# Later eviction of the sum banks that share a tile, stores on GpSimd's queue, and V's bound in two steps, in a fused attention and expert-layer kernel

## The chip, the cores and the metric

The kernel runs on one core of a Trainium2 chip. The metric is the device time of one execution in microseconds (us). TensorE (PE) does the matrix products, VectorE (DVE) and ScalarE (ACT) everything elementwise, SyncE (SP) and GpSimd (POOL) issue transfers. Each engine works through its own list of instructions in order, and waits on semaphores for the others.

## The reference

```python
def _attn_ref(q, k, v, proj):                      # 4 batches, 8 heads, 768 rows, 64 columns
    q_bits = (np.einsum('bhsd,dk->bhsk', q, proj) > 0)
    k_bits = (np.einsum('bhsd,dk->bhsk', k, proj) > 0)
    mask = q_bucket[:, :, :, None] == k_bucket[:, :, None, :]
    scores = np.where(mask, scale * np.matmul(q, k.transpose(0, 1, 3, 2)), -1000000000.0)
    attn = np.exp(scores - np.max(scores, axis=-1, keepdims=True))
    attn = attn / (np.sum(attn, axis=-1, keepdims=True) + 1e-09)
    return np.matmul(attn, v)

def _moe_ref(x, w_in, w_out):                      # 3072 x 512, 512 x 2048, 2048 x 512
    h = x @ w_in
    g = np.where(h > 0.0, h, np.exp(np.minimum(h, 0.0)) - 1.0)
    return g @ w_out
```

The attention's output, heads side by side, is the input of the two products. The weights are 64-bit floats in memory and are decoded by the kernel.

## The kernel before

**Tiling.** The rows of a batch make two chunks of 384 rows (three blocks of 128), eight chunks in all. Heads go in four pairs. A slot of the main loop is one query tile: 128 rows of one head, so a pair has six slots in a chunk, a chunk 24, a batch 48. Every number that enters a product is split into a high and a low half in float16, and three products replace one.

**One slot.** PE makes the scores of a query tile (`s`, L507, four matmuls). DVE copies them out with their row maximum (`pt`, L519); only then is the one score tile `s` free again. For each two query tiles ACT makes the exponentials (L535) and the high half of the normalised rows (`hl`, L143), DVE the low half (L152), and SP issues transfers that transpose them into `PT` (L550). Some slots later PE multiplies them with V (`av`, L558). In the steps of the loop that are due then, ACT, DVE and SP also prepare Q, K and V for later pairs; the bits of the buckets come from small products (`z`, L286).

**The two weight products run one chunk behind, between the scores.** `moe_stream` yields one matmul at a time. `first` makes `h` for 128 of the 2048 inner columns (f = 0 to 15; 12 matmuls, L584); ACT and DVE make `U`, the activated halves (L595, L598, L599, L143, L152). `second` adds one f to the sums of the chunk's three row blocks (L620, three matmuls for each block). The sums are in three PSUM banks for the whole chunk: `o[0]` and `o[1]` are the two halves of one tile named `o`, `o[2]` is a tile of its own, `o2`. After the last f, each block's sum is scaled into an SBUF tile `ot`, a slice of `W` (`W<-o` in the profile; the first and third block on ACT at L143, the second on DVE at L145), and stored to `out_dram` (L632). There are two `ot` slices for the three blocks, so the third block's copy waits until the first block's store has landed.

**What orders the work.** PE's list is the order in which the code is written. ACT's, DVE's and SP's lists are set by a scheduler that places each instruction by priority; the copies of the sums have high priority. Instructions that touch one tile in conflict are ordered by the tile, not by the half of it.

**V's bound.** For each batch after the first, V is loaded, its four parts are squared and summed on ACT (L207), and one step `scale` takes the largest sum (L411, DVE), multiplies it with ones on PE to spread it over partitions (`sum<-vx`, L184), and makes a scale from it in five small DVE instructions (L186 to L199). Four steps `split` then write V's halves (`vhl`, two instructions on ACT, two on DVE each). The steps are due at slots counted from the batch's first slot.

Of the kernel before, what the change touches and what calls it, by code (L numbers as in the profile page):

```python
# [19 lines left out]
V_TOP = 13  # L20
# [46 lines left out]
def lsh_attention_moe(  # L67
# [55 lines left out]
    def part(name):  # L123

        n = taken.get(name, 0)
        taken[name] = n + 1
        return area[name][n % len(area[name])]
# [43 lines left out]
    def behind_max():  # L171
        return tc.issue_after(latest[-1].ins) if latest else nullcontext()

    def powers(mx, n, floor, top, tag, pool=None, rows=False, squares=False, ex=None):

        pool = pool or small  # L180
        mall = pool.tile([P, n], F32, tag=tag + "m", name=tag + "m")
        if not rows:
            t = ps_a.tile([P, 512], F32, tag="av", name="sum")[:, :n]
            nc.tensor.matmul(t, ones, mx.bitcast(BF16).rearrange("p (n t) -> p n t", t=2)[:, :, 1], start=True, stop=True)  # L184
            mx = t
        nc.vector.tensor_scalar(mall, mx, floor, None, ALU.max)  # L186
        if ex is None:
            ex = pool.tile([P, n], F32, tag=tag + "e", name=tag + "e")
        if squares:

            nc.vector.tensor_scalar(
                ex.bitcast(I32), mall.bitcast(I32), 1, 0x7F800000, ALU.logical_shift_right, ALU.bitwise_and
            )
            nc.vector.tensor_scalar(ex, ex, 2.0**64, None, ALU.mult)
        else:
            nc.vector.tensor_scalar(ex.bitcast(I32), mall.bitcast(I32), 0x7F800000, None, ALU.bitwise_and)
        sc = pool.tile([P, n], F32, tag=tag + "s", name=tag + "s")
        nc.vector.reciprocal(sc, ex)
        nc.vector.tensor_scalar(sc, sc, 2.0**top, None, ALU.mult)  # L199
        return ex, sc  # L200
# [182 lines left out]
    def prep_v(b):  # L383
        st = {"f": [], "v": [None] * NP}

        def load():
            mx = small.tile([P, NP], F32, tag="vx", name="vx")
            for p in range(NP):
                f = vpool.tile([P, 2, NC, D], F32, tag="v", name="vf")
                with tc.issue_after(ks[b, V_AFTER]["done"].ins) if b == 0 else nullcontext():  # L390
                    nc.sync.dma_start(
                        f.rearrange("p h c d -> p h (c d)"),
                        v[b, 2 * p : 2 * p + 2].rearrange("h (p c) d -> p h (c d)", c=NC),
                    )
                st["f"].append(f)
            st["mx"] = mx
            if b == 0:
                for p in range(NP):
                    sums(p)

        def sums(p):
            f = st["f"][p]
            squares(st["mx"][:, p : p + 1], f.rearrange("p h c d -> p (h c d)"), steady.k1 if b else junk0)

        def scale():
            with behind_max():
                bound()

        def bound():
            m1 = small.tile([P, 1], F32, tag="vx1", name="vx1")  # L410
            nc.vector.tensor_reduce(m1, st["mx"], axis=AX.X, op=ALU.max)  # L411
            st["ex"], st["sc"] = powers(m1, 1, 2.0**-34, V_TOP, "v", squares=True)

        def split(p):
            f = st["f"][p]
            t = vpool.tile([P, 2, NC, 2, D], F16, tag="v", name="vhl")
            st["v"][p] = t
            for j in range(2):
                scaled("v_hi", t[:, j, :, 0, :], f[:, j], st["sc"])
                rest("v_lo", t[:, j, :, 1, :], f[:, j], st["sc"], t[:, j, :, 0, :])  # L420

        parts = [lambda p=p: sums(p) for p in range(NP)] if b else []
        return st, [load] + parts + [scale] + [lambda p=p: split(p) for p in range(NP)]


    wst = {}
# [145 lines left out]
    def moe_stream(chunks):  # L572
# [33 lines left out]
        def second(c, f, g16):  # L606
            n = c["nc"]
            if f == 0:
                if not banks:
                    two = ps_o.tile([P, 2, 512], F32, tag="o", name="o")  # L610
                    banks.extend([two[:, 0], two[:, 1], ps_o.tile([P, 512], F32, tag="o2", name="o2")])
                c["o"] = banks[:n]
                c["os"] = small.tile([P, 1], F32, tag="os", name="os", bufs=2)
                nc.vector.scalar_tensor_tensor(
                    c["os"], vs[c["b"]][0]["ex"], 2.0 ** (G_DOWN - V_TOP - 2 * W_TOP), wst["e2"], ALU.mult, ALU.mult
                )
            o = c["o"]
            for t in range(n):
                for i, (gx, wx) in enumerate(((0, 0), (0, 1), (1, 0))):
                    nc.tensor.matmul(  # L620
                        o[t][:, :DO],
                        g16[:, gx, t * P : (t + 1) * P],
                        WH[:, NSI + 1 + f, wx, :],
                        start=f == 0 and i == 0,
                        stop=f == NF - 1 and i == 2,
                    )
                    if f == NF - 1 and i == 2:
                        rows = out[c["b"] * S : (c["b"] + 1) * S, :].rearrange("(p c) o -> p c o", c=NC)
                        ot = part("ot")
                        with tc.high_priority():  # L630
                            scaled("out", ot, o[t][:, :DO], c["os"])
                        nc.sync.dma_start(rows[:, c["c0"] + t, :], ot)  # L632
                    yield DO

        for c in chunks:
# [140 lines left out]
        vs[b] = prep_v(b)  # L776
    for b in range(1, B):
        s0 = [c for c in chunks if c["b"] < b][-1]["end"]
        vdue += [(s0 + x, s) for x, s in zip((-16, -14, -13, -12, -11, -9, -8, -2, 4, 10), vs[b][1])]


    wq = list(wsplits)
# [50 lines left out]
    def weights(n):  # L833
        nonlocal w_credit, w_at
        w_credit += n
        while w_credit >= 1:

            at = (w_at + (2 if w_at >= NSI else 1)) * SL
            users = {x[1] for x in due} | ({"v"} if len(vdue) == NP + 2 + (B - 1) * (2 * NP + 2) else set())
            if any(a < at + SL and at < z and users & u for a, z, u in guards):  # L840
                break
            if w_at not in w64 and w_at < NSI + NSO:
                break
            w_credit -= 1
            if w_at >= W_SPLIT and NSI not in split_done and len(split_done) < KT:
                split_w()
            elif w_at < NSI + NSO:
                wdecode(w_at)
                w_at += 1
                load_w()  # L850
                if w_at in (NSI, NSI + NSO):
                    wscale(w_at // (NSI + NSO))
            elif wq:
                split_w()
# [97 lines left out]
```

## Time and profile before

| | |
|---|---|
| median of 3 runs | 966.19 us (963.73 to 966.58) |
| the profiled execution | 964.54 us |
| its span, first to last instruction | 962.7 us |
| PE, ACT, DVE busy | 825.0, 742.0, 705.7 us |
| mean granted clock of PE | 0.95 |

The profile is of one execution, and its span is 1.84 us shorter than its own time. A group of instructions is named by its line, its engine and its tiles, out<-in. "Idle before" is the time in which the engine had nothing to do ahead of the instruction, with the instruction whose end released it. "PEclk" is the share of full speed that PE's clock was granted.

### The profile page before, as it was taken

The page shows a single profiled execution, that of the slowest core. Times are in us where ns is not written, and L with a number is a line of the kernel's source. Part 1 is how long each engine was busy: PE and PEld are TensorE (multiplying, and loading weights), DVE is VectorE, ACT ScalarE, POOL GpSimd, SP SyncE. Part 2 cuts the span into 40 slices and gives each one's busy share as a digit, 9 for nine tenths or more (in the row PEclk, how much of TensorE's full clock was granted, in tenths as well). Part 3 has the DMA queues.
Part 4 walks back from the last instruction along what each step waited for, and adds up shares of the span by engine and source line. Part 5 has one row for each costly group of instructions (what it writes and reads, how often), then busy time and mean ns, then how long its engine had stood idle before and what let it go on. Part 6 is the DMA issues. An engine that isn't in the chain of part 4 may idle for free.

```text
span 962.7 us, 14525 instructions
## 1 busy us (share of the span) xinstructions
PE 825.0 (86%) x4975; PEld 422.4 (44%) x4975; DVE 705.7 (73%) x1528; ACT 742.0 (77%) x1469; POOL 2.6 (0%) x25
## 2 busy tenths in 40 slices
PE   2536555879989999889989998989989999999997
PEld 0113222434445555444545554544545454555453
DVE  6789899898877777678767686687877687665232
ACT  5667777999879787789779797698878788786443
POOL 1000000000000000000000000000000000000000
PEclk9998665999999999899999999999999999999999
DMA  9999988676886759486887666785786767656000
GB/s 284 264 201 215 223 213 179 131 151 139 158 177 151 151 107 144 97 186 120 166 188 135 127 130 122 136 165 102 143 168 126 125 116 149 100 99 99 33 1 33
DMA packets 406121, 138.46 MB, mean 144 GB/s; under 512 B 380960, under 2 KB 398880, under 8 KB 406048
## 3 DMA queue, kind: packets, MB, share of 16 engines
q1 hardware_dynamic: 405888, 137.54, 69.4%
q8 instruction: 39, 0.64, 0.3%
q14 instruction: 34, 0.28, 0.1%
q10 hardware_dynamic: 160, 0.00, 0.0%
HBM read 35.65 MB, written 6.29 MB: 44 GB/s over the span
## 4 chain that ended last, share of the span: by engine, by line
PE 55%; DVE 16%; DMA 15%; ACT 8%; issue 4%; SPq 1%; ACTq 0%; DVEq 0%
PE o L620 18%; PE h L584 18%; PE av L558 9%; PE s L507 7%; DVE pt L519 4%; DMA O<-nat1q 3%; DVE hl L152 3%; DMA K<-natk 3%; DMA PT<-hl 3%; ACT pt L535 3%; PE z L286 2%; ACT W L143 1%; DMA W<-in_moe_w_in_dram 1%; DVE U L152 1%; DVE natk L152 1%
## 5 line engine op out<-in xcount | busy, mean ns | idle before, releaser
L620 PE MATMUL o<-W,U 128*128 128x512 f16 x1152 | 283.8, 384 | 20.0 <-ACT W L143 20.0
L584 PE MATMUL h<-x,W 128*128 128x384 f16 x1536 | 284.1, 329 | 0.0
L584 PEld LDWEIGHTS <-W 128*128 128x128 f16 x1536 | 148.2, 98 | 123.8 <-issue 24.0
L519 DVE TENSOR_SCALAR_CACHE_REDUCE pt<-s 128x768 f32<-128x768 f32 x177 | 168.2, 950 | 42.8 <-PE s L507 41.6
L535 ACT ACTIVATE pt<-pt,nb,sg 128x768 f32<-128x768 f32 x192 | 195.3, 1019 | 1.8
L152 DVE SCALAR_TENSOR_TENSOR hl<-pt,r,hl 128x768 f16<-128x768 f32 x192 | 189.9, 1011 | 9.2 <-ACT hl L143 8.9
L143 ACT ACTIVATE hl<-pt,r 128x768 f16<-128x768 f32 x192 | 168.6, 926 | 32.7 <-DVE r L545 32.1
L620 PEld LDWEIGHTS <-U 128*128 128x128 f16 x1152 | 111.8, 98 | 141.6 <-issue 28.4
L507 PE MATMUL s<-K,O 128*128 128x384 f16 x708 | 152.7, 339 | 19.0 <-DVE pt L519 15.1
L558 PE MATMUL av<-PT,vhl 128*64 128x384 f16 x1152 | 114.9, 353 | 26.4 <-DMA PT<-hl 13.7
L599 DVE SCALAR_TENSOR_TENSOR U<-U 128x384 f32<-128x384 f32 x128 | 70.8, 553 | 79.5 <-ACT U L598 79.2
L507 PEld LDWEIGHTS <-O 76*128 76x128 f16 (+1 forms) x768 | 74.8, 102 | 120.5 <-issue 42.1
L595 ACT ACTIVATE U<-h,ch 128x384 f32<-128x384 f32 x128 | 73.1, 571 | 66.8 <-PE h L584 66.3
L152 DVE SCALAR_TENSOR_TENSOR U<-U,sgg 128x384 f16<-128x384 f32 x128 | 78.4, 613 | 53.8 <-ACT U L143 53.8
L558 PEld LDWEIGHTS <-vhl 128*64 128x64 f16 x1152 | 73.2, 118 | 80.4 <-issue 16.3
L143 ACT ACTIVATE U<-U,sgg 128x384 f16<-128x384 f32 x128 | 77.8, 608 | 25.5 <-DVE U L599 25.4
L598 ACT ACTIVATE U<-h,ch 128x384 f32<-128x384 f32 x128 | 72.9, 570 | 0.0
L471 PE MATMUL acc<-W,ones 128*128 128x512 bf16 x32 | 17.0, 547 | 34.8 <-DVE W L468 33.9
L535 ACT ACTIVATION_READ_ACCUMULATOR pt<-pt,nb,sg 128x1 f32 x192 | 36.3, 189 | 0.0
L291 DVE TENSOR_SCALAR zb<-z,pjt 64x384 f16<-64x384 f32 (+1 forms) x48 | 29.1, 606 | 6.9 <-PE z L286 6.9
L532 ACT ACTIVATE nb<-m,sg 128x2 f32<-128x2 f32 x96 | 27.7, 288 | 5.4 <-DVE pt L519 4.9
L286 PE MATMUL z<-O,pjz 64*32 64x384 f16 (+1 forms) x192 | 27.5, 363 | 2.4 <-DVE w0m L186 1.7
(102 smaller groups left out, 502.7 us busy)
## 6 DMA issues: line engine op xcount, KB each, us to landing
U<-in_moe_w_in_dram SPq DMA_DIRECT2D x12, 512.0 KB
vf<-in_v_dram SPq DMA_DIRECT2D x16, 384.0 KB
U<-in_moe_w_out_dram SPq DMA_DIRECT2D x12, 512.0 KB
out_dram<-W SPq DMA_DIRECT2D x24, 256.0 KB
qst<-in_q_dram SPq DMA_DIRECT2D x30, 192.0 KB
kst<-in_k_dram SPq DMA_DIRECT2D x14, 384.0 KB
PT<-hl SPq DMA_TRANSPOSE x192
W<-in_moe_w_in_dram SPq DMA_DIRECT2D x4, 512.0 KB
```

The lines of the kernel that those rows point to most:

```text
L143: nc.scalar.activation(o, x, AF.Copy, scale=s)
L152: nc.vector.scalar_tensor_tensor(o, x, s, hi, ALU.mult, ALU.subtract)
L286: nc.tensor.matmul(t[u * QD : (u + 1) * QD], pj["z"][:rows, x, :], mv, start=n == 0, stop=n == len(ways) - 1)
L507: nc.tensor.matmul(s_tile[:, n, :HALF], st[o][:rows, at, :], kst[kk][:rows, j * NC + n * HC : j * NC + (n + 1) * HC, :].rearrange("p a b - ...
L519: top = nc.vector.tensor_scalar(pt.rearrange("p (n e) -> p n e", n=2), s_tile[:, :, :HALF], CLAMP, None, ALU.max, ALU.max, accum_out=duo[0 ...
L535: nc.scalar.activation(pt, pt, AF.Exp, bias=nb[:, n : n + 1], scale=st["sg"][:, 0:1], accum_out=sm[:, n : n + 1])
L558: nc.tensor.matmul(av[j * D : (j + 1) * D], vt[:, j, c, vx, :], PTs[j][:, :, px, c, :], start=n == 0, stop=n == last,)
L584: nc.tensor.matmul(h, WH[:, g * KT + t, wx, fc * P : (fc + 1) * P], c["xs"][t][:, xx, :], start=n == 0, stop=n == 3 * KT - 1,)
L595: nc.scalar.activation(e, h, AF.Exp, scale=c["ch"])
L598: nc.scalar.activation(hp, h, AF.Relu, scale=c["ch"])
L599: nc.vector.scalar_tensor_tensor(e, e, -1.0, hp, ALU.add, ALU.min)
L620: nc.tensor.matmul(o[t][:, :DO], g16[:, gx, t * P : (t + 1) * P], WH[:, NSI + 1 + f, wx, :], start=f == 0 and i == 0, stop=f == NF - 1 and ...
```

## The change

```diff
         def scale():
             with behind_max():
-                bound()
-
-        def bound():
-            m1 = small.tile([P, 1], F32, tag="vx1", name="vx1")
-            nc.vector.tensor_reduce(m1, st["mx"], axis=AX.X, op=ALU.max)
-            st["ex"], st["sc"] = powers(m1, 1, 2.0**-34, V_TOP, "v", squares=True)
+                st["ex"], st["sc"] = powers(st["m1"], 1, 2.0**-34, V_TOP, "v", squares=True)
...
+        def top():
+            m1 = small.tile([P, 1], F32, tag="vx1", name="vx1")
+            with behind_max():
+                nc.vector.tensor_reduce(m1, st["mx"], axis=AX.X, op=ALU.max)
+            st["m1"] = m1
...
-        return st, [load] + parts + [scale] + [lambda p=p: split(p) for p in range(NP)]
+        return st, [load] + parts + ([top, scale] if b else [lambda: (top(), scale())]) + [lambda p=p: split(p) for p in range(NP)]
...
-                    if f == NF - 1 and i == 2:
-                        rows = out[c["b"] * S : (c["b"] + 1) * S, :].rearrange("(p c) o -> p c o", c=NC)
-                        ot = part("ot")
-                        with tc.high_priority():
-                            scaled("out", ot, o[t][:, :DO], c["os"])
-                        nc.sync.dma_start(rows[:, c["c0"] + t, :], ot)
+                    if f == NF - 1 and i == 2 and (t > 0 or n == 1):
+                        for u in range(t + 1) if t < 2 else (2,):
+                            rows = out[c["b"] * S : (c["b"] + 1) * S, :].rearrange("(p c) o -> p c o", c=NC)
+                            ot = part("ot")
+                            with tc.high_priority():
+                                scaled("out", ot, o[u][:, :DO], c["os"])
+                            nc.gpsimd.dma_start(rows[:, c["c0"] + u, :], ot)
...
-        vdue += [(s0 + x, s) for x, s in zip((-16, -14, -13, -12, -11, -9, -8, -2, 4, 10), vs[b][1])]
+        vdue += [(s0 + x, s) for x, s in zip((-16, -14, -13, -12, -11, -9, -7, -5, 1, 6, 11), vs[b][1])]
...
-            users = {x[1] for x in due} | ({"v"} if len(vdue) == NP + 2 + (B - 1) * (2 * NP + 2) else set())
+            users = {x[1] for x in due} | ({"v"} if len(vdue) == NP + 2 + (B - 1) * (2 * NP + 3) else set())
```

The first block's sum is no longer copied out between the last matmuls of the first block and those of the second: both are copied after the second block's last matmul, the third after its own. All 24 stores are issued by POOL instead of SP. The step that takes V's largest sum stays nine slots ahead of the batch; the product with ones and the scale follow two slots later, and the four splits are due at slots -5, 1, 6 and 11 instead of -8, -2, 4 and 10.

At the end of the fourth chunk, ACT's list around the copies of the sums (`W<-o`: the copy from tile `o`; `W<-o_1559`: from tile `o2`; `U`: the activated halves; `hl`, `r`, `nb`, `pt`: the query tiles) was:

```order
L207 ACTIVATE nat1q,qx<-qst 128x384
L143 ACTIVATE hl<-pt,r 128x768 x2
L143 ACTIVATE W<-o,os 128x512
L143 ACTIVATE U<-U,sgg 128x384
L532 ACTIVATE nb<-m,sg 128x2
L535 ACTIVATE pt,sm<-pt,nb,sg 128x768 x2
L544 ACTIVATE r<-sm 128x2
L143 ACTIVATE hl<-pt,r 128x768 x2
L595 ACTIVATE U<-h,ch 128x384
L598 ACTIVATE U<-h,ch 128x384
L143 ACTIVATE W<-o_1559,os 128x512
```

and is now, from the same `nat1q` on:

```order
L207 ACTIVATE nat1q,qx<-qst 128x384
L143 ACTIVATE hl<-pt,r 128x768 x2
L143 ACTIVATE U<-U,sgg 128x384
L143 ACTIVATE W<-o,os 128x512
L533 ACTIVATE nb<-m,sg 128x2
L536 ACTIVATE pt,sm<-pt,nb,sg 128x768 x2
L596 ACTIVATE U<-h,ch 128x384
L599 ACTIVATE U<-h,ch 128x384
L545 ACTIVATE r<-sm 128x2
L143 ACTIVATE W<-o_1559,os 128x512
L596 ACTIVATE U<-h,ch 128x384
L599 ACTIVATE U<-h,ch 128x384
```

The copy of the first sum stays where it was, but for one instruction; a pair of `U` instructions now stands ahead of the second `hl` pair, and so does the copy from `o2`. On DVE at the same place (`W<-o`: the copy of the second block's sum; `zb`: bits of the buckets) before:

```order
L519 TENSOR_SCALAR pt,m<-s 128x768
L152 SCALAR_TENSOR_TENSOR hl<-pt,r,hl 128x768 x2
L152 SCALAR_TENSOR_TENSOR U<-U,sgg 128x384
L145 TENSOR_SCALAR W<-o,os 128x512
L291 TENSOR_SCALAR zb<-z,pjt 64x384
L545 RECIPROCAL r<-r 128x2
L519 TENSOR_SCALAR pt,m<-s 128x768
```

and now:

```order
L520 TENSOR_SCALAR pt,m<-s 128x768
L152 SCALAR_TENSOR_TENSOR hl<-pt,r,hl 128x768
L291 TENSOR_SCALAR zb<-z,pjt 64x384
L152 SCALAR_TENSOR_TENSOR hl<-pt,r,hl 128x768
L152 SCALAR_TENSOR_TENSOR U<-U,sgg 128x384
L145 TENSOR_SCALAR W<-o,os 128x512
L520 TENSOR_SCALAR pt,m<-s 128x768
```

`zb` moved ahead of the copy, and the next score tile is taken right behind it, ahead of a reciprocal. PE's list is the same in both kernels, except for the product of V's largest sum with ones. For the third batch it stood inside the twelve matmuls of one `h`:

```order
L584 MATMUL h<-x_3447,W 128x384
L184 LDWEIGHTS ones
L184 MATMUL sum<-vx_4260,ones 128x1
L584 LDWEIGHTS W
L584 MATMUL h<-x_3447,W 128x384
```

and stands now 72 matmuls later, after the next `av`, two score tiles and an `h`:

```order
L621 MATMUL o<-W,U 128x512
L184 LDWEIGHTS ones
L184 MATMUL sum<-vx_4260,ones 128x1
L621 LDWEIGHTS U
L621 MATMUL o<-W,U 128x512
```

On DVE the maximum itself keeps its place, behind the same score tile; only what follows the product moved back by some ten instructions.

## Prediction

> **What bounds the kernel now.** The page comes first, for the span and the engines' shares:
>
> ```profile
> span 962.7 us, 14525 instructions
> ...
> PE 825.0 (86%) x4975; PEld 422.4 (44%) x4975; DVE 705.7 (73%) x1528; ACT 742.0 (77%) x1469; POOL 2.6 (0%) x25
> ...
> PEclk9998665999999999899999999999999999999999
> ```
>
> No engine is full over the whole span, so the share alone decides nothing. The view of stretches, asked for the time between two chunk ends, does:
>
> ```profile
> 302.00:384.00 82.00, 82.00 (x525) 44.33 (x520) 61.35 (x131) 67.54 (x136) 0.00 (x0) 1.00 0.75 132
> ```
>
> The columns are the stretch, its length, then PE, weight loads, DVE, ACT and POOL busy, PE's clock, the DMA share and GB/s. PE is busy in all 82.00 us at full clock; ACT lacks 14.5 us and DVE 20.7. There PE is the bound, and what it loses elsewhere it can't win back here. So the waits of PE after the start-up, 200 us to the end, are what a change can gain:
>
> ```profile
> PE o L620 <- ACT W L143: 20.0, 8, 5.2
> PE s L507 <- DVE pt L519: 9.9, 15, 1.2
> PE sum L184 <- DVE vx L411: 9.2, 3, 3.9
> PE av L558 <- DMA PT<-hl: 3.6, 2, 2.1
> PE av L558 <- DMA O<-zb: 2.0, 1, 2.0
> ```
>
> These are total, times and longest. The first is the second block's matmuls held by the copy of the first block's sum, once in each chunk; the third is the product with V's largest sum, once for each batch after the first. Together they are 29.2 of 44.7 us, and the change aims at both. They cost more than their idle time. Of the half-clock stretches after 200 us, every one begins during such a wait or just behind it:
>
> ```profile
> 213.66:220.49 6.83, 5.87 (x28) 2.67 (x29) 5.55 (x15) 6.36 (x13) 0.00 (x0) 0.50 0.94 249
> ...
> 387.75:394.57 6.82, 5.00 (x16) 1.53 (x16) 4.36 (x8) 4.79 (x10) 0.00 (x0) 0.50 0.69 141
> ...
> 599.37:606.20 6.83, 5.68 (x18) 1.83 (x18) 3.69 (x6) 5.14 (x11) 0.00 (x0) 0.50 0.83 138
> ...
> sum 34.12, PE 30.18 PEld 11.33 DVE 23.78 ACT 28.37 POOL 0.00; mean PE 4.31 PEld 1.62 DVE 3.40 ACT 4.05 POOL 0.00
> ```
>
> Seven stretches hold 30.18 us of PE's work at a clock of 0.50, so half of it, 15.1 us, is lost beside the 29.2: 2.9 in the first, 2.5 and 2.8 in the other two long ones, and 1.7 in each of four short ones ((30.18 - 5.87 - 5.00 - 5.68) / 4 / 2). The Trainium skill, TensorE: Matmul & The Clock Gate, Part 1, says that the clock halves after an idle window of about 3.4 us. The trace agrees on the lengths (6.83 is twice 3.41) but not on the trigger: the wait of 2.67 us shown below brought a half-clock stretch too. By that rule only the three waits over 3.4 us would return clock time, 8.2 us in place of 15.1.
>
> **The change, term by term.** The sum goes against the profiled execution, 964.54 us, of which 962.7 is its span. PE's list loses and gains no work.
>
> *Two long waits at chunk ends* (second and fourth chunk). The fourth:
>
> ```profile
> 595.69 0.65 PE L507 MATMUL s<-K,O 128*128 128x384 f16 x3
> 600.52 2.72 PE L620 MATMUL o<-W,U 128*128 128x512 f16 x6 [4.18 <-ACT W L143]
> 603.17 1.25 PE L286 MATMUL z<-O,pjz 128*32 128x384 f16 x6
> 604.36 2.36 PE L584 MATMUL h<-x,W 128*128 128x384 f16 x8
> 606.56 0.81 PE L507 MATMUL s<-K,O 128*128 128x384 f16 x4
> ...
> 609.81 0.81 PE L507 MATMUL s<-K,O 128*128 128x384 f16 x4
> 610.46 2.75 PE L620 MATMUL o<-W,U 128*128 128x512 f16 x12
> ...
> 596.19 0.52 ACT L207 ACTIVATE nat1q<-qst 128x384 bf16<-128x384 f32 x1 [1.66 <-DMA O<-nat1q]
> ...
> 599.79 0.68 ACT L143 ACTIVATE W<-o,os 128x512 f32<-128x512 f32 x1
> ...
> 611.66 0.29 ACT L532 ACTIVATE nb<-m,sg 128x2 f32<-128x2 f32 x1
> ...
> 599.13 1.94 DVE L152 SCALAR_TENSOR_TENSOR hl<-pt,r,hl 128x768 f16<-128x768 f32 x2
> ...
> 607.41 0.96 DVE L519 TENSOR_SCALAR_CACHE_REDUCE pt<-s 128x768 f32<-128x768 f32 x1 [2.25 <-PE s L507]
> ```
>
> The durations of the kinds of instructions that stand in the two lists, from the groups of the page (count, then busy time and mean ns of one):
>
> ```profile
> L143 ACT ACTIVATE hl<-pt,r 128x768 f16<-128x768 f32 x192 | 168.6, 926 | 32.7 <-DVE r L545 32.1
> ...
> L535 ACT ACTIVATE pt<-pt,nb,sg 128x768 f32<-128x768 f32 x192 | 195.3, 1019 | 1.8
> ...
> L595 ACT ACTIVATE U<-h,ch 128x384 f32<-128x384 f32 x128 | 73.1, 571 | 66.8 <-PE h L584 66.3
> L152 DVE SCALAR_TENSOR_TENSOR U<-U,sgg 128x384 f16<-128x384 f32 x128 | 78.4, 613 | 53.8 <-ACT U L143 53.8
> ...
> L291 DVE TENSOR_SCALAR zb<-z,pjt 64x384 f16<-64x384 f32 (+1 forms) x48 | 29.1, 606 | 6.9 <-PE z L286 6.9
> ```
>
> PE is free at 596.3. ACT, late by a transfer, copies the sum only at 599.79. After the change PE goes on: six matmuls at the 0.23 us of the last PE row, the `z` products and eight `h` at full clock (half of 1.25 and of 2.36) and the score matmuls (0.65), done near 600.2 where they started at 606.56. Then DVE decides: behind the score tile that ends at 599.1 its new list has `hl` twice (1.9), `zb` 0.6, `U` 0.6 and the copy 0.7 (as on ACT), so it takes the next score tile near 603.0, not 607.41, and PE's next scores start near 604.0, not 609.81: 5.8 us sooner. ACT gains less. Behind the copy at 599.79 come one `U` (0.6), `nb` (0.3) and two exponentials (2.0), to 603.3 as before; then two pairs of `U` (2.2), the small `r` (I take 0.2), the third copy (0.7), one more `U` (0.6) and two `hl` (1.8), done near 608.8. Before, it came to the same point (`nb`) at 611.66. That is 2.9 us. PE can't stay ahead of ACT for long, but ACT has slack afterwards; between 2.9 and 5.8 I take the middle, 4.3, for each: **8.6 us**. The bounds are nothing, where a later wait eats it, and the whole of both: idle 5.24 (the row below) and 4.18, half clock 2.5 and 2.8, 14.7.
>
> ```profile
> 389.57 2.72 PE L620 MATMUL o<-W,U 128*128 128x512 f16 x6 [5.24 <-ACT W L143]
> ```
>
> *Five short waits at chunk ends.* 20.0 less 5.24, 4.18 and the 0.78 of the last chunk leaves 9.8; two of the four short half-clock stretches (1.7 each) follow them, so 13.2 at most. At these ends ACT is not late by a transfer, the copy merely stands behind a few instructions of its list, and nothing PE needs next (score tile, `h` bank) is near its limit. I take the middle of 9.8 and 13.2, **11.5 us**; the low bound is half of 9.8, where ACT is behind.
>
> *V's bound.* The product waits for a maximum that stands behind a score tile on DVE:
>
> ```profile
> 428.26 0.15 DVE L411 TENSOR_REDUCE vx<-vx 128x1 f32<-128x4 f32 x1
> ...
> 428.46 0.16 PE L184 MATMUL sum<-vx,ones 128*128 128x1 bf16 x1 [2.67 <-DVE vx L411]
> ...
> 626.00:668.00 42.00, 37.25 (x221) 18.45 (x219) 34.92 (x72) 38.17 (x78) 0.00 (x0) 0.96 0.77 147
> ...
> L143 ACT ACTIVATE vhl<-vf,vs 128x384 f16<-128x384 f32 x32 | 17.5, 602 | 0.1
> ```
>
> With 72 matmuls in between, the maximum is long there, and the wait goes: 9.2 us idle and 6.3 of half clock (2.9 + 1.7 + 1.7) over three batches, 15.5 at most. But here ACT is behind: in the 42 us around the third of these waits it is busy for 38.17, and the second `av` after it already waits about 2 us for `PT` (the last rows of the waits above). PE would only arrive there sooner and wait longer; what counts is how much sooner `hl` is made. In the new list four of the eight `vhl` copies on ACT stand behind the `hl` pair that this `av` needs, and each costs 17.5 / 32 = 0.55 us: 2.2 us for each batch, **6.6 us**. Low bound zero (the late splits push the next `hl` instead), high 15.5. The product moves behind an `av` whose copy must clear the same PSUM buffer; about 30 matmuls lie between, which I cost at nothing.
>
> *Stores on POOL.* POOL has 2.6 us of work in the whole kernel, so nothing queues there but the stores themselves. SP loses 24 issues and the waits ahead of them, and no PE wait but the two `av` rows (5.6 us together) hangs on SP: bounds 0 and 5.6, taken as 0, since those follow a late `hl`. What POOL takes to issue is in no row. It matters in two places. First, the third copy on ACT waits for the first store to land; in the fourth chunk's new list some 3.7 us of other ACT work lie between. Second, the end:
>
> ```profile
> 956.16 0.69 ACT L143 ACTIVATE W<-o,os 128x512 f32<-128x512 f32 x1 [2.18 <-PE o L620]
> 956.87 3.15 SPq L632 DMA_DIRECT2D out_dram<-W  x3
> 956.90 1.46 PE L620 MATMUL o<-W,U 128*128 128x512 f16 x6 [0.78 <-ACT W L143]
> ...
> 958.98 0.69 ACT L143 ACTIVATE W<-o,os 128x512 f32<-128x512 f32 x1 [2.13 <-DMA out_dram<-W]
> ...
> 1.33 5.33 DMA pf<-in_proj_dram
> ```
>
> The first store takes 958.98 - 956.87 = 2.1 us; the last copy is held by it, and the last store ends the span. Now the first copy waits for the second block's three matmuls, 0.65 us, so the same chain ends 0.65 later, and twice by what POOL's issue adds: nothing at best, 5.33 - 2.1 = 3.2 us at worst by the slowest small transfer of the trace. I take 0.4 each, near the rows of the same store: **1.5 us lost**, bounds 0.65 and 7.
>
> The Trainium skill, DMA: Bandwidth & Descriptors, Latency and other measured facts, gives about 1 us to the first byte for a transfer issued by GpSimd against 0.6 for SP. No run here shows it yet; by it the loss would be 0.65 + 0.8, the same 1.5.
>
> **Sum.** 8.6 + 11.5 + 6.6 - 1.5 = 25.2 us: 939.3 for an execution like the profiled one. The median of the runs shown is 1.65 above it, which makes 941.
>
> **Rivals.** (1) *ACT and DVE take over as the bound.* PE's waits move to `s`, `av` and `h`. For it: ACT's 38.17 of 42 us. Against: the 82 us in which ACT lacks 14.5. Half of the short waits (4.9), ACT's 2.9 at each long one and no gain at V, less 1.5, is 9.2: 957. (2) *All comes back*, idle time and half clock: 14.7 + 13.2 + 15.5 - 0.65 = 42.8: 923. Against it stand the busy engines around V. (3) *Slower: ACT is held at the third copy.* ACT's list is in order, and behind that copy stand `U` and `hl`, for which PE waits. If a store from POOL lands 3.7 us after the first copy, nothing happens; each microsecond beyond is lost eight times. With the 25.2 to use up and 2.9 to be seen as slower, it decides from 3.7 + 28.1 / 8 = 7.2 us on; at 9 us the loss is 42 and the time 983. For it: no row shows POOL's issue. The Trainium skill, SBUF — State Buffer, Who interferes with whom, speaks against the change here: some DVE instructions lock GpSimd out of the port by which it writes descriptors. By the longest DVE instructions quoted here, 0.97 us each (half of the `hl` row's 1.94), one such lock costs a microsecond, not four. (4) *No change:* the list that the scheduler made anew puts another wait on PE, worth the gain, 966.
>
> **Chances.** The forecast 0.70, from 930 to 951; (1) 0.15; (2) 0.05; (3) 0.05; (4) 0.05. What measurement tells from no change is 0.3%, 2.9 us. Faster: 0.70 + 0.15 + 0.05 = 0.90; within 0.3% 0.05; slower 0.05. The range takes in the forecast, (1) and part of (2): 925 to 958.
>
> **What would show it.** Right: no wait of `o L620` for `ACT W`, none of `sum L184`; half-clock stretches at chunk ends short or gone; waits of `av` on `PT` grown around V; ACT's third copy waiting for `out_dram` under 1 us; the last store 0.65 to 2 us later after the last matmul than now. Wrong: a new PE wait of several us at `s` or `h` behind each chunk end (1), or a gap of ACT ahead of the third copy in each chunk (3).

## The result and the profile after

The changed kernel takes 951.25 us, median of four runs (948.24 to 956.71), beside 965.97 for the kernel before. The ratio is 0.9848, 95% interval 0.9822 to 0.9873: 14.7 us faster, where 25 were forecast. The time lies in the stated range; the size is 0.6 of the forecast. For two kernels below, V's bound alone and joint copies alone, the profiled execution was a slow one (1438 and 2114 us), so of these only the times of their fast runs are used, and of the second also the order of ACT's list.

The profiled execution of the changed kernel took 948.24 us, of which 946.5 is its span. Its page, the same lines as shown of before:

```profile
span 946.5 us, 14531 instructions
...
PE 818.4 (86%) x4975; PEld 420.4 (44%) x4975; DVE 704.0 (74%) x1528; ACT 739.3 (78%) x1469; POOL 15.7 (2%) x49
...
PEclk9956666998999999999999999999999999999998
```

The waits of PE from 200 us to the end (total, times, longest):

```profile
PE s L508 <- DVE pt L520: 21.5, 24, 3.5
PE av L559 <- DMA PT<-hl: 10.0, 7, 3.1
PE o L621 <- ACT W L143: 3.1, 4, 1.6
```

The two waits at which the change aims went as forecast: `o` for ACT's copy from 20.0 us to 3.1, `sum` for the maximum from 9.2 to none. But `s` for DVE grew from 9.9 to 21.5 and `av` for its transfers from 5.6 (two rows before) to 10.0. Of the 26.1 us removed from the two waits, 16.0 came back in two others. The half-clock stretches:

```profile
210.88:214.29 3.41, 3.36 (x22) 1.99 (x24) 3.01 (x5) 3.36 (x8) 0.00 (x0) 0.50 0.88 154
231.36:238.18 6.82, 5.33 (x18) 1.87 (x19) 6.36 (x13) 6.82 (x13) 0.00 (x0) 0.50 0.36 66
449.81:453.22 3.41, 3.41 (x23) 1.74 (x19) 0.63 (x2) 1.48 (x4) 0.00 (x0) 0.50 0.25 89
sum 13.64, PE 12.10 PEld 5.60 DVE 10.01 ACT 11.67 POOL 0.00; mean PE 4.03 PEld 1.87 DVE 3.33 ACT 3.89 POOL 0.00
```

Three instead of seven, 12.10 us of PE's work instead of 30.18, so 6.1 us lost instead of 15.1. All three lie where V is prepared; at the chunk ends none is left. (Behind the last matmul both kernels have one, which costs nothing.)

PE issues the same matmuls for the scores, `av`, `h` and `o` in both kernels, so the start of the same matmul can be compared. The table follows how far the changed kernel is ahead, worked out from the two traces, and what each part of the program added (negative is faster; before rounding). Its rows are the starts of the 1st, 253rd, 1045th and 1152nd sum matmul and, for V and for the chunks 2 to 4, of the 265th, 457th, 553rd, 649th, 745th and 817th `av` matmul. The two spans differ by 16.2 us.

```
part of the program                          before    after     difference  added
first sum matmul                             179.66    175.77     -3.9       -3.9
V for the second batch                       270.75    267.74     -3.0       +0.9
end of chunk 1 (short wait)                  365.43    361.11     -4.3       -1.3
end of chunk 2 (long wait)                   403.84    394.48     -9.4       -5.0
V for the third batch                        482.81    475.30     -7.5       +1.9
end of chunk 3 (short)                       559.27    552.81     -6.5       +1.0
end of chunk 4 (long)                        615.12    603.32    -11.8       -5.3
V for the fourth batch                       670.84    657.37    -13.5       -1.7
ends of chunks 5, 6, 7 (short)               916.39    897.50    -18.9       -5.4
last sum matmul (chunk 8)                    957.98    938.15    -19.8       -0.9
end of the span                              962.7     946.5     -16.2       +3.6
```

The first row is no part of the change: two later executions with the same lists in that stretch came to the first sum matmul at 176.7 and 180.5. What is left, 12.3 us: the long waits gave 10.4, the short ones 5.7 and the last chunk 0.9, V took 1.1, the end took 3.6. So some 4 of the 16.2 us between the two spans are chance.

The end, the last copies and stores of the changed kernel (start, duration, engine, idle before):

```profile
937.92 0.69 ACT L143 ACTIVATE W<-o,os 128x512 f32<-128x512 f32 x1 [2.83 <-PE o L621]
938.64 0.75 DVE L145 TENSOR_SCALAR W<-o,os 128x512 f32<-128x512 f32 x1 [2.90 <-ACT W L143]
938.90 0.54 POOL L635 DMA_DIRECT2D out_dram<-W  x1 [54.23 <-ACT W L143]
939.68 0.54 POOL L635 DMA_DIRECT2D out_dram<-W  x1 [0.25 <-DVE W L145]
941.32 0.69 ACT L143 ACTIVATE W<-o,os 128x512 f32<-128x512 f32 x1 [2.72 <-DMA out_dram<-W]
942.30 0.54 POOL L635 DMA_DIRECT2D out_dram<-W  x1 [2.08 <-ACT W L143]
```

The first copy now starts 0.2 us before the last sum matmul instead of 1.8. From its end the third copy waits 2.7 us for the store, and the span ends 4.5 us behind the third copy; with SP these were 2.1 and 3.0.

### The profile page after: what moved, and what is told of

Read it like the earlier page. It is cut to its first block, busy times and chain, and to the rows that moved or that the text cites. A ratio compares the mean times of both kernels' runs of the same rounds, so it can differ in the third digit from the quotient of the medians.

```text
span 946.5 us, 14531 instructions
## 1 busy us (share of the span) xinstructions
PE 818.4 (86%) x4975; PEld 420.4 (44%) x4975; DVE 704.0 (74%) x1528; ACT 739.3 (78%) x1469; POOL 15.7 (2%) x49
## 4 chain that ended last, share of the span: by engine, by line
issue 50%; DVE 14%; PE 14%; DMA 13%; ACT 6%; SPq 1%; POOL 1%; POOLq 0%; ACTq 0%; DVEq 0%
PE o L621 4%; PE av L559 4%; PE h L585 3%; DVE pt L520 3%; DMA PT<-hl 3%; DVE hl L152 3%; PE s L508 2%; DMA K<-natk 2%; DMA O<-nat1q 2%; ACT pt L536 2%; DMA W<-in_moe_w_in_dram 1%; DMA U<-in_moe_w_out_dram 1%; DVE W L469 1%; POOL out_dram L635 1%; DVE W L479 1%
## 5 line engine op out<-in xcount | busy, mean ns | idle before, releaser
L621 PE MATMUL o<-W,U 128*128 128x512 f16 x1152 | 280.2, 380 | 3.2 <-ACT W L143 3.1
L585 PE MATMUL h<-x,W 128*128 128x384 f16 x1536 | 279.8, 326 | 0.0
L207 ACT ACTIVATE nat1q<-qst 128x384 bf16<-128x384 f32 x30 | 15.5, 516 | 18.1 <-DMA O<-nat1q 16.0
```

The costliest lines, as they stand in the source:

```text
L585: nc.tensor.matmul(h, WH[:, g * KT + t, wx, fc * P : (fc + 1) * P], c["xs"][t][:, xx, :], start=n == 0, stop=n == 3 * KT - 1,)
L621: nc.tensor.matmul(o[t][:, :DO], g16[:, gx, t * P : (t + 1) * P], WH[:, NSI + 1 + f, wx, :], start=f == 0 and i == 0, stop=f == NF - 1 and ...
```

## The experiments

All ratios are to the kernel before, with a 95% interval.

**The parts of the change.** The first kernel has only V's bound of the change.

> The kernel before with V's bound in two steps and the new split slots, evictions and stores as before. Theory A (from the profile of the changed kernel: V's part gained nothing, since DVE idles 2.5 us at zb ahead of a ready score tile near 228 and the splits of V start some 6 us later): the three waits of sum for the maximum (9.2 us) go, as much comes back at s and av within 40 us, and the time is 0 to 3 us from the kernel before: 963 to 968. Theory B (V gains what was predicted and something else loses it in the full change): 6.6 us faster, near 959.

966.9 us, ratio 0.9985 (0.9962 to 1.0008): no change that can be told, in theory A's range.

The next has all but that part: V's bound in one step, its splits in the old slots.

> The changed kernel with V's bound in one step as before: evictions together, stores from GpSimd. Theory A: V's part is worth nothing, so this is within 3 us of the changed kernel (951). Theory B: it is 6.6 us slower, near 958.

953.61 us, ratio 0.9875 (0.9840 to 0.9909). Beside 0.9848 for the full change, V's part is worth 2.6 us on top of the others; the two intervals overlap, so this isn't told from nothing either. The time lies in theory A's range. The waits of PE (from 200 us on) show what the two steps trade:

```profile
PE s L507 <- DVE pt L519: 21.5, 28, 2.5
PE sum L184 <- DVE vx L411: 9.3, 3, 3.9
PE av L558 <- DMA PT<-hl: 4.8, 3, 2.1
PE o L620 <- ACT W L143: 1.2, 3, 0.6
```

Without the two steps `sum` waits 9.3 us, and `av` 4.8; with them `sum` not at all and `av` 10.0. More than half of what goes at `sum` comes back at `av`.

Then the stores. Back on SP in the full change:

```diff
-                            nc.gpsimd.dma_start(rows[:, c["c0"] + u, :], ot)
+                            nc.sync.dma_start(rows[:, c["c0"] + u, :], ot)
```

> The changed kernel with its stores on SP's queue again. Theory A (the late landing of GpSimd's stores, 4.3 to 5.0 us where SP needs 2.1, holds ACT's third copy 8.0 us in all, behind it DVE 6.0 us, and PE 3.1 us at o and some 5 us at s): ACT's wait for out_dram falls under 4 us, the end is 2 us shorter, and the time is 4 to 8 us under the changed kernel, 943 to 947. Rival (SP's queue is blocked by its own waits, so that stores leave late): the first store of a chunk leaves SP over 3 us after its copy, ACT waits as long as now, time within 2 us of 951.

957.85 us, ratio 0.9906 (0.9874 to 0.9938): 5.6 us slower than with GpSimd, where theory A had 4 to 8 faster. The two intervals only just part, and two of the six runs (952.2 and 952.9) lie where the changed kernel does. ACT's wait for `out_dram` fell from 8.0 to 3.9 us, as theory A said, and the time rose all the same, so theory A falls. The rival has the place, a store that leaves SP late, but neither the size nor a wait of ACT as long as now. SP's list at the end of the first chunk, then PE's and ACT's:

```profile
291.68 3.29 SPq L551 DMA_TRANSPOSE PT<-hl  x2
295.07 1.33 SPq L635 DMA_DIRECT2D out_dram<-W  x2
...
295.88 1.46 PE L621 MATMUL o<-W,U 128*128 128x512 f16 x6
299.46 1.50 PE L621 MATMUL o<-W,U 128*128 128x512 f16 x6 [2.12 <-ACT W L143]
...
291.33 0.67 ACT L143 ACTIVATE W<-o,os 128x512 f32<-128x512 f32 x1
...
298.21 0.62 ACT L143 ACTIVATE U<-U,sgg 128x384 f16<-128x384 f32 x1
298.72 0.69 ACT L143 ACTIVATE W<-o,os 128x512 f32<-128x512 f32 x1
```

The first copy is done at 292.0, but its store leaves SP at 295.07, behind two transposes that wait for `hl`. ACT's third copy has no wait of its own: it stands late in ACT's list, at 298.72, 7.4 us behind the first. At this chunk end the third copy's place is the only thing that differs between the two lists of ACT. That the scheduler expects the store on SP late, and so puts other work ahead, is the likely reason; no run shows it. The same place with GpSimd:

```profile
286.30 0.68 ACT L143 ACTIVATE W<-o,os 128x512 f32<-128x512 f32 x1
...
292.08 0.69 ACT L143 ACTIVATE W<-o,os 128x512 f32<-128x512 f32 x1 [0.54 <-DMA out_dram<-W]
...
287.29 0.67 POOL L635 DMA_DIRECT2D out_dram<-W  x1 [283.80 <-ACT nb L533]
...
292.82 1.45 PE L621 MATMUL o<-W,U 128*128 128x512 f16 x6 [0.52 <-ACT W L143]
```

The store leaves 0.3 us behind the copy, the third copy stands 5.8 us behind the first, and PE waits 0.52 instead of 2.12 for the bank that it frees. Over the kernel with stores on SP:

```profile
PE o L621 <- ACT W L143: 13.6, 6, 3.0
```

This is 13.6 us against 3.1. So with stores on SP the joint copies move the wait from the second sum to the third, in the next chunk, and with GpSimd's stores most of it goes. Two kernels test this from the other side: the kernel before with its stores on GpSimd and nothing else, and the kernel before with joint copies and nothing else.

> The kernel before with its 24 stores issued by GpSimd and nothing else; PE's list is the same, ACT's and DVE's differ at three chunk ends. Theory A (what POOL's stores win over SP's in the changed kernel, 951 against 958, is that the scheduler can put the third copy early, which matters only where the next chunk's first sum matmul waits for it): here that wait is not there, the waits of o for ACT (20.0 us) stay, the end grows by 1 to 2 us: 965 to 969. Rival (taking stores out of SP's queue lets loads and transposes leave sooner, wherever the copies stand): 3 to 6 us faster, 960 to 963.

968.44 us, ratio 1.0042 (1.0021 to 1.0063): slower by 4.1 us. The waits of `o` stay (18.9 us in eight), and from the last sum matmul to the end it takes 6.7 us instead of 4.7. Theory A.

> The kernel before with the first two sums copied together after the second, V's bound and SP's stores as before. Theory A (joint copies and GpSimd's stores are worth little apart and 12 us together, since with SP the third copy stands later and PE waits 2 us at o for it, six times in the run with stores on SP): the 20.0 us of waits of o shrink to about 13, 4 to 8 us faster than before, 958 to 962. Rival (joint copies alone bring the gain): 953 to 956.

958.08 us, median of four runs, ratio 0.9922 (0.9890 to 0.9955): 7.5 us faster. Theory A. So joint copies give 7.5, GpSimd's stores cost 4.1, and both together give 12.1 (the ratios 0.9922, 1.0042 and 0.9875 on 966 us): 8.7 us belong to the two jointly and to neither alone, give or take 5 by the three intervals. The order of ACT's list bears this out in part. Between the first copy and the third stand 6, 11, 6, 11, 4 and 11 other instructions (reads of accumulators left out) at the ends of chunks 1 to 6 with joint copies alone, and 9, 6, 8, 6, 7 and 6 with GpSimd's stores as well. So with joint copies alone the third copy stands late at three ends of six; in the full change with stores on SP it does at all six, behind 11 or 12.

**The store that lands late.** With GpSimd the stores land 2.3 to 5.3 us after their issue (median 4.0):

```profile
DMA to landing us min/median/max: 2.3/4.0/5.3
```

That is the view of the output tensor. ACT waits for them, first in the kernel before (stores on SP), then in the changed kernel, with a wait of DVE that follows:

```profile
ACT W L143 <- DMA out_dram<-W: 8.3, 3, 3.4
...
ACT W L143 <- DMA out_dram<-W: 8.0, 6, 2.7
...
DVE os L615 <- ACT W L143: 6.0, 5, 1.4
```

The total is no larger than before; it is spread over six chunk ends instead of three. DVE's small `os` stands behind that third copy, since the scale of the next chunk but one reuses the buffer; so the wait goes on to DVE. To take that link away:

```diff
-                c["os"] = small.tile([P, 1], F32, tag="os", name="os", bufs=2)
+                c["os"] = small.tile([P, 1], F32, tag="os", name="os", bufs=8)
```

> The changed kernel with eight buffers for the scale os instead of two, so that DVE's os does not wait for the third copy two chunks earlier in the ring; nothing else in any engine's list moves. If DVE's 6.0 us behind the third copy are what PE loses at s behind chunk ends, 3 to 5 us under the changed kernel, 946 to 948. If ACT's own lateness is what PE waits for, within 1.5 us of it.

950.29 us, ratio 0.9847 (0.9808 to 0.9886): DVE's 6.0 us are gone, the time is the same. PE's wait for `s` is 21.7 as before. The link costs nothing. The other link, ACT's own wait, was taken away where a stage buffer is idle:

```diff
-                            ot = part("ot")
+                            if u == 2 and (c["c0"] == 0 or c is chunks[-1]):
+                                ot = stg.tile([P, DO], F32, tag="k", name="ot3", bufs=2)
+                            else:
+                                ot = part("ot")
```

> The changed kernel with a buffer of its own for the third copy of five chunks (the first of each batch and the last), taken from the idle stage of the keys, so that this copy does not wait for the first store to land. Theory A (the wait of ACT for out_dram, 8.0 us in six, holds PE at o, 3.1 us, and at s behind chunk ends): at these ends the waits go, 3 to 5 us under the changed kernel, 946 to 948. Theory B (ACT has other work that PE needs as soon, so an earlier third copy only moves the wait; eight buffers for os gained nothing either): within 2 us of 951, apart from the end, where the last copy no longer waits for the first store, 2 us.

956.41 us, ratio 0.9907 (0.9876 to 0.9939): ACT's wait falls from 8.0 to 3.2 us and the kernel is 5 us slower. ACT's list was made anew, with the third copy two rows behind the first. PE's waits:

```profile
PE s L508 <- DVE pt L520: 19.6, 23, 3.9
PE av L559 <- DMA PT<-hl: 19.1, 10, 4.1
PE o L621 <- ACT W L143: 0.3, 1, 0.3
```

The wait of `o` is gone, `av` waits 19.1 instead of 10.0. An earlier third copy is no gain by itself. The trace shows what stands against it. At three of the five chunk ends concerned (the first, third and fifth of the kernel) the first transpose of `hl` leaves as soon behind the first copy as in the changed kernel (0.4 us), but now all three stores leave within 1.9 us, beside the transposes. The third store lands 6.5, 7.5 and 7.7 us after its issue instead of 2.4, 2.3 and 2.8, and the `av` that needs the transposes goes on 9.6, 10.6 and 10.8 us behind the first copy, where the changed kernel's went on at 8.5, 9.1 and 8.4. The edit also takes a buffer from the stage of the keys, and three loads of keys leave 12 to 15 us later. What each of the two costs isn't separated, and because this run changes the lists and the wait together, it doesn't price the late landing alone.

**The end.** The last chunk's stores on SP; no other list moves.

```diff
-                            nc.gpsimd.dma_start(rows[:, c["c0"] + u, :], ot)
+                            (nc.sync if c is chunks[-1] else nc.gpsimd).dma_start(rows[:, c["c0"] + u, :], ot)
```

> The changed kernel with the last chunk's three stores on SP, the other 21 on GpSimd; no other list moves. By the traces the end of the changed kernel holds two stores in a row from GpSimd (2.7 us and 4.5 us behind their copies) where SP needed 2.1 and 3.0: 2.0 us less, 949. If the landing is slow for another reason than the issuing engine, within 0.5 us of the changed kernel.

951.06 us, ratio 0.9845 (0.9800 to 0.9890): the 2.0 us expected don't show in the time, which can't tell so little. In the trace:

```profile
944.18 0.69 ACT L143 ACTIVATE W<-o,os 128x512 f32<-128x512 f32 x1 [2.83 <-PE o L621]
944.89 3.21 SPq L635 DMA_DIRECT2D out_dram<-W  x3
...
947.06 0.69 ACT L143 ACTIVATE W<-o,os 128x512 f32<-128x512 f32 x1 [2.19 <-DMA out_dram<-W]
```

The third copy follows 2.2 us behind the end of the first, not 2.7. From the last sum matmul to the end of the span: before 4.7, this 7.2, the changed kernel 8.3; all stores on SP 6.3, GpSimd's alone 6.7. By the two pairs that change all stores, GpSimd's issue costs 2.0 at the end (8.3 less 6.3, 6.7 less 4.7), and the later first copy 1.6; the two add up to the 3.6 of the table. But this edit, the direct test, takes back 1.1 and not 2.0, and why its end is 0.9 longer than with all stores on SP isn't shown.

**V's slot.** The scale one query tile earlier, ahead of 19 matmuls of the 72 that it was moved, and with it the four splits one to three slots earlier:

```diff
-        vdue += [(s0 + x, s) for x, s in zip((-16, -14, -13, -12, -11, -9, -7, -5, 1, 6, 11), vs[b][1])]
+        vdue += [(s0 + x, s) for x, s in zip((-16, -14, -13, -12, -11, -9, -8, -7, -2, 4, 10), vs[b][1])]
```

> The changed kernel with V's scale one query tile earlier (the product with the maximum moves ahead of 18 matmuls, the copies of V on ACT move up with it). Theory A (V's part gained nothing since its copies start 6 us later than before, so that hl and the probabilities come later): 2 to 5 us faster than the changed kernel, 946 to 949, with fewer waits of av. Theory B (ACT is full there, 38 of 42 us, so the order of its work gains nothing): within 1.5 us of 951.

948.59 us, ratio 0.9838 (0.9802 to 0.9874), in theory A's range, and `av` waits 8.5 us instead of 10.0, in seven places as before; but the times alone don't tell it from the changed kernel. The stretch from the first sum matmul to the last leaves out the scattered start and the end. The view of the sum matmuls gives first and last start; for the changed kernel:

```profile
L621 PE MATMUL o<-W,U x1152: 376/379/634, 175.8 to 938.1; 128*128 128x512 f16 x192
```

And with the earlier slot:

```profile
L621 PE MATMUL o<-W,U x1152: 376/379/631, 179.0 to 937.6; 128*128 128x512 f16 x192
```

That is 762.4 us against 758.6. With V's slots as in the change it took 761.5 (eight `os`) and 763.9 (end on SP) in two other executions; with the earlier slot 757.0 and 760.8 in two executions below, which carry the edits of `os` and of the end as well. Most is gained while V is prepared for the second batch, where the table's +0.9 becomes -2.0. The reason there lies in DVE's list. In the changed kernel:

```profile
227.99 0.62 DVE L291 TENSOR_SCALAR zb<-z,pjt 128x384 f16<-128x384 f32 x1 [2.46 <-PE z L286]
...
231.83 0.95 DVE L520 TENSOR_SCALAR_CACHE_REDUCE pt<-s 128x768 f32<-128x768 f32 x1
...
225.39 0.81 PE L508 MATMUL s<-K,O 128*128 128x384 f16 x4
...
232.85 1.46 PE L508 MATMUL s<-K,O 128*128 128x384 f16 x4 [3.50 <-DVE pt L520]
```

The score tile is ready at 226.2. DVE stands idle for 2.46 us at `zb`, which waits for PE, and takes the score tile only at 231.83; PE then stops for 3.50 us, and a long half-clock stretch follows. With the earlier slot:

```profile
227.88 0.95 DVE L520 TENSOR_SCALAR_CACHE_REDUCE pt<-s 128x768 f32<-128x768 f32 x1
...
231.70 0.61 DVE L291 TENSOR_SCALAR zb<-z,pjt 128x384 f16<-128x384 f32 x1
```

The score tile stands ahead of `zb`, and the long stop is gone. In exchange the product waits for the PSUM buffer of the `av` ahead of it (`sum` for DVE's `x`, 4.0 us in three), the cost that the prediction had put at nothing in the later slot, where it is nothing.

**A version that beats both.** The earlier slot, eight buffers for `os`, the last chunk's stores on SP and its third copy in a buffer of its own (the edit above, with `c is chunks[-1]` alone as its condition):

> The changed kernel with V's scale one query tile earlier, eight buffers for os, the last chunk's stores on SP, and its third copy in a buffer of its own. Theory A (what the single runs show adds up, measured from the first sum matmul to the last: 3.8 for V's scale, 0.9 for os, and at the end 1.2 for SP and 2.2 for the wait that goes): 7 us under the changed kernel, 943 to 945. Theory B (each of these is noise of one execution): 949 to 952, but for 2 to 3 us at the end.

944.97 us, ratio 0.9791 (0.9739 to 0.9842). With the own buffer at five chunk ends in place of one:

> As the run before, with the third copy in a buffer of its own at five chunk ends, not at the last alone. If the wait of the third copy for the store holds PE: 2 to 3 us under the run before, 941 to 943. If not: within 1 us of it, or slower, where the stage's buffer delays a load of keys.

948.71 us, ratio 0.9828 (0.9783 to 0.9872): 3.7 us slower by the medians, as for the buffer alone, though the intervals overlap. The first of the two again:

> The kernel with V's scale one query tile earlier, eight buffers for os, and the last chunk's stores on SP with a buffer of its own for the third copy, run again with more rounds. If its gain over the changed kernel is real: 943 to 947, its whole interval under that of the changed kernel (0.9822 to 0.9873). If the first runs were lucky: 948 to 951.

945.23 us, ratio 0.9776 (0.9756 to 0.9797), clear of the changed kernel's interval: 21.6 us faster than before (0.0224 of 966), some 7 more than the change.

## Why the prediction was right in direction and too large

**The bound.** Right: PE's waits set the time, the two named waits went, and the clock stretches at the chunk ends went with them.

**Two long chunk-end waits, 8.6 forecast.** 10.4 in the profile, 10.3 and 11.4 in the two other executions with these chunk ends. The replay of DVE's and ACT's lists put the gain of each between 2.9 and 5.8; 5.0 and 5.3 came. Right, but only with GpSimd's stores: with stores on SP the same two ends gave 5.5.

**Five short chunk-end waits, 11.5 forecast.** 5.7, and 3.7 and 4.9 in the two others: near the low bound, 4.9. This is the first term that was mis-sized. The step that failed is "nothing PE needs next (score tile, `h` bank) is near its limit". At the ends of chunks 5, 6 and 7 it holds; they gave 5.4 of the 5.5 us waited there. At chunks 1 and 3, the two with a half-clock stretch, it doesn't: of 7.7 us at most (2.05 and 2.22 of wait, 1.7 each of clock) they gave 0.3. Within 50 us of the end of chunk 1 PE waited another 1.7 us in four places. At chunk 3 PE went on 2.2 us sooner, then waited for DVE's score tiles and for the third copy:

```profile
PE s L508 <- DVE pt L520: 3.3, 4, 1.4
PE o L621 <- ACT W L143: 1.6, 1, 1.6
```

This is the window 486 to 553. The first of the four waits for score tiles, 0.54 us, was there before too (493.27); the other three, 2.8 us, are new, as is the wait for the third copy. In the same stretch before (496 to 560) the 2.2 us at `o` were the only wait. What was gained is given back within 60 us. That is rival (1), at two chunk ends instead of everywhere.

**V's bound, 6.6 forecast.** Nothing alone, and 2.6 with the rest, not clear of noise. The step that failed is "what counts is how much sooner `hl` is made", worked out from four copies of V that leave ACT's list ahead of one `av`. The list was made anew as a whole, and a new order on DVE (`zb` ahead of a ready score tile) cost 3.5 us and a half-clock stretch at the second batch alone. The slot decided more than the split in two: with scale and splits earlier, the stretch between the sum matmuls is 3.8 us shorter (means of 758.8 and 762.6, three executions each; which of the two moves gave it isn't separated). The 1.1 us that V's rows of the table lose are not V's part alone: with V's bound in one step the same rows lose 1.7.

**Stores on GpSimd, 1.5 lost forecast.** The end took 3.6 from the last sum matmul on, while that matmul itself came 0.9 sooner, since the last chunk's wait of 0.78, which the forecast had set aside, went. That is 2.7 lost: 0.7 for the later first copy, as forecast (0.65), and 2.0 for the stores, where 0.8 had been taken. In the body it was the other way: GpSimd's stores gained 5.6 us net over SP's in the full change, so some 7.6 ahead of the end. The step that failed is "no PE wait but the two `av` rows (5.6 us together) hangs on SP: bounds 0 and 5.6, taken as 0". It looked at what waits for SP before, and not at where the store would stand in SP's list and where the third copy would then stand in ACT's. The two errors, at V and at the stores, have opposite signs, and this is luck: with its stores on SP the same kernel gains 9 us of the 25, and it is an order of ACT's list that the forecast had at nothing which brings the total near 15. The Trainium skill, SBUF — State Buffer, Who interferes with whom, had been weighed as a reason for late stores from GpSimd; the landing was late in the body and 2.3 at the quiet end, which alone would fit. The traces speak for another cause, the transfers of the other queue (last section), and no run shows that the landing set the time.

**The clock.** By the Trainium skill's idle window of about 3.4 us (TensorE: Matmul & The Clock Gate, Part 1) 8.2 us of clock time would return; all 15.1 were counted in the upper bounds. 9.0 returned net (15.1 less 6.1), but not by the length of single waits. Two waits of the changed kernel:

```profile
210.93 4.75 PE L559 MATMUL av<-PT,vhl 128*64 128x384 f16 x35 [2.48 <-DMA PT<-hl]
...
655.56 1.65 PE L559 MATMUL av<-PT,vhl 128*64 128x384 f16 x18 [2.08 <-DMA PT<-hl]
```

The first, of 2.48 us, is followed by the half-clock stretch from 210.88 on; the second, of 2.08, by none. What decides is how a wait lies on a fixed grid. In each trace here the half-clock stretches start at multiples of 3.41 us from one another. The grid steps in which these two waits fall, with PE's busy time behind the comma:

```profile
207.46:210.88 3.42, 0.99 (x5) 0.21 (x3) 3.37 (x8) 3.42 (x8) 0.00 (x0) 1.00 0.85 174
651.20:654.61 3.41, 2.28 (x13) 0.99 (x10) 3.41 (x9) 3.41 (x9) 0.00 (x0) 1.00 1.14 210
654.61:658.02 3.41, 2.46 (x30) 1.73 (x32) 3.41 (x6) 3.41 (x6) 0.00 (x0) 1.00 0.12 27
```

The first wait falls into one step, of which PE is busy 0.29; the second is shared by two, with 0.67 and 0.72. Over the twelve traces used here, from 200 us to 12 us before the end, all 40 full-clock steps in which PE was busy for less than 0.40 were followed by half clock, 4 of the 14 between 0.40 and 0.50, and none of some 2490 above. So the wait of 2.05 us at the first chunk end of the kernel before cost clock time, and one of 3.50 us, split by the grid (at 237.6 in the run with the last stores on SP), did not. Why a step under 0.40 is followed by half clock isn't shown; the shares are those of the profile.

**The rivals.** The slower one, ACT held at the third copy, had its mechanism: ACT waits 0.5 to 1.3 us at five chunk ends and 2.7 at the last, as the 3.7 us of cover and a landing 4.5 to 5.1 us behind the copy say. It stayed far under the 7.2 from which it would decide, and the link to DVE cost nothing when it was cut. Rival (1) came nearer than its chance of 0.15 says: two of its three terms are what was measured (half of the short waits, nothing at V), and only the long waits went as the forecast had it. The time of 951.25 lies at the edge between the two, since the forecast's own share ran from 930 to 951.

## What to carry to other kernels

A wait removed on the bounding engine is worth what stands behind it: replay the next 60 us of the other engines' lists, at each place, before adding it up. Its clock time depends on how much of one 3.41 us step it empties. Where a scheduler makes the lists, an edit that frees one queue (here SP) can be worth more through the order that it allows than through the queue itself, and only with the edit that needs that order. Time single parts, and both of a pair together: here +4.1 and -7.5 made -12.1.

## What was not expected of the hardware

A store issued by GpSimd took 0.54 us of its engine and landed 2.3 us after issue at the quiet end. In the body the first two stores of a chunk took 3.8 to 5.4 us, but the third of chunks 1 to 4 again 2.3 to 2.4, though issued at most 5.2 us behind the second. What goes with it is the traffic of the other queue, and not how busy DVE is. Over the 228 GpSimd stores of ten traces, take the 2.3 us from the issue: where the packets of the other (SP's) queue filled less than 0.15 of the 16 DMA engines' time, the median landing was 2.3 us (94 stores), also for the 31 during which DVE was busy over 0.65 of that time; where they filled 0.45 or more, it was 4.6 (129 stores, three of them under 3.0), and 4.4 to 5.2 for the 22 with DVE busy under 0.6. Nine of the 94 landed after 3.8 to 4.7 all the same, eight of them the third store of chunk 6; why isn't shown. On SP the store at the end took 2.1.

Executions with the same lists differ by 4.7 us before the first sum matmul (175.8, 176.7, 180.5), in a stretch where the DMA engines load weights and inputs. A comparison of two profiled spans here is good to some 5 us; the stretch behind it repeats to 2.4 (761.5 to 763.9).
